# Loads of a fused RWKV and SoLU kernel moved from one DMA queue to three

## The chip, the cores and the metric

The kernel runs on one core of a Trainium2 chip. The metric is the time of one launch on the device in microseconds. Over the two runs of the kernel before, it is 154.34 us (median; 154.29 and 154.40).

Five engines work side by side, each through its own list of instructions, in order: PE (TensorE, matrix products), DVE (VectorE), ACT (ScalarE), POOL (GpSimd) and SP (SyncE). SP computes nothing here; it issues DMA transfers between the device memory and the on-chip memory. An engine waits at an instruction until the semaphores that it names have been reached, and everything behind it on that engine waits too.

## The reference

Two stages, in float32. First a recurrence over 768 positions for 4 batches and 8 heads of width 48:

```python
for t in range(S):
    cur = np.einsum('bhd,bhe->bhde', u[None] * kt, vt)
    y[:, :, t] = np.einsum('bhd,bhde->bhe', rt, state + cur)
    state = wt[:, :, :, None] * state + np.einsum('bhd,bhe->bhde', kt, vt)
```

Then, with `x` the 3072 x 384 rows of `y`, a hidden layer of 1024 with SoLU, a norm over its columns, and the way back to 384:

```python
h = x @ w_in
sm = softmax(h)             # over the 1024 columns
solu = h * sm
ln = (solu - mean(solu)) / np.sqrt(var(solu) + 1e-06) * g_ln
out = ln @ w_out
```

## The kernel before

The 768 positions are cut into 6 chunks of 128, so with 4 batches there are 24 units of work, numbered 0 to 23 (`units`, chunk by chunk). For a unit the four inputs w, k, r and v are each loaded as a tile of 128 positions by 8 heads by 48 numbers in float32: 192 KB, in rows of 192 bytes, 1024 rows to a tile.

All work is written out by hand in the string `ORDER` (lines 21 to 67). A word is a stage, a unit and sometimes a letter or digit that says which engine or PSUM bank: `vb3.p` is the stage `vb` of unit 3 on POOL. Each word calls a function, and the wrapper `InOrder` (lines 72 to 90) makes the instructions of each engine follow one another in just the order in which the words stand. Line 86 in that wrapper is where nearly every instruction is recorded, so the profile gives L86 for nearly all; a group is told by its tiles.

The words that matter here:

- `LW`, `LK`, `LR`, `LV` (lines 246 to 256) load w, k, r, v of a unit, all on SP. `LU`, `LG`, `LI`, `LO` load u, g and the two weight matrices; `out` (line 536) stores a finished unit. v has 7 buffers (`NIO`), unit i taking buffer i modulo 7.
- `lw` (ACT) takes the logarithm of w; `cum` (PE) sums it along the chunk; `ex` (ACT) takes exponents; `kp` (DVE, `scaled` at line 333) multiplies k and r with them.
- `p` and `q` (POOL) multiply k with r and with u; `qh` (POOL) halves q by an addition for some units; `dg` (DVE) sums q per head; `dv` (POOL) multiplies that sum with v.
- `vb` (POOL, ACT or DVE by its letter) casts v to bfloat16. It is the only reader of a loaded v tile.
- `M`, `m`, `sel`: scores on PE, their copy on ACT or DVE, the mask of some units on POOL. `Y` (PE) and `y` (ACT or DVE) make the output of the recurrence out of m, vb, dv and the state; `S`, `et`, `st` carry the state on.
- `X`, `xT`, `H`, `e`, `he`, `hq`, `ea`, `Oa`, `Ob`, `sq`, `qm`, `lv`, `o`: the second stage; `ea` (POOL) adds the two halves of e.
- `gw`, `ce`, `mn`, `mc`, `wi`: the weights, once.

How the readers of v stand: for units 3, 4, 6, 7, 10, 12 and 14 `vb` is on POOL; for 5, 8, 11 and 13 on DVE; for 9 on ACT. In `ORDER` the word `LV` of a unit stands ahead of its `vb`, often directly ahead: `LV3 vb3.p dv3 sel4`, `LV4 vb4.p`, `LV14 vb14.p`. Where `LV` is on SP that closeness means little, since SP goes through its own words ahead of the others.

Of the kernel before, what the change touches and what calls it, by code (L numbers as in the profile page):

```python
# [8 lines left out]
F32 = mybir.dt.float32  # L9
BF16 = mybir.dt.bfloat16  # L10
# [11 lines left out]
LW2 LU0 ik0 lw2 hot5.4 cum2.0 LW1 lw1 us0.7 ih0 LW3 lw3 cum3.2 LR2 uc0 ex2 LK2 p2 LV2 vb2.p kp2 hot4.4 krk2.6 krr2  # L22
LR1 LK1 cum1.4 LW0 ex1 kp1 kr2.d hot1.0 S2.7 lw0 et2 LV1 vb1.d LW4 st2 p1 q1 hot2.0 krk1.1 krr1 q2 qh2 dg2 LG0
kr1.a M2.4 ex3 hot1.0 M1.6 m1.d dv2 LR0 LK0 p0 q0 cum0.0 ex0 lw4 cum4.6 ex4 kp0 krk0.1 krr0 LR3 gs0.0 gc0 dg1
m2.d Y2.i0 kr0.d LK3 p3 LR4 LV0 vb0.a dg0 dv1 kp3 Y1.i5 hot3.1 krk3.4 krr3 LK4 kp4 M0.2 m0.d krk4.1 y1.a X1.5
krr4 y2.a X2.0 dv0 xT2.d hot1.6 Y0.n7 y0.d kr3.a M3.2 hot1.0 X0.6 S1.4 p4 q3 kr4.a xT1.a xT0.a LI2 LI1 wi1.a
M4.0 m4.a et1 LI0 S0.5 et0 wi0.d m3.d LO1 wi2.p H1.6 e1 gw5.a H2.0 e2 H0.2 LO0 gw2.a q4 qh4 dg4 qh3 dg3 gw4.p
gw7.p LV3 vb3.p dv3 sel4 LW6 e0 gw6.d st1 LV4 vb4.p he1 lw6 dv4 gw1.d LW5 gw0.d gw3.d mn0.4 mc0 ce5.p ce6.p
Y3.i7 ce4.p he2 st0 he0 cum6.0 y3.a ce7.p hot1.5 X3.6 lw5 xT3.a ce3.d LK6 LR6 p6 Y4.n5 LR5 LK5 ce2.d hq0.a ex6
LW7 cum5.2 H3.6 p5 y4.d ex5 ce1.d ce0.d Oa0.5 kp6 krk6.1 krr6 S4.0 hq1.d Oa1.4 kp5 krk5.3 krr5 X4.2 Ob1 e3 he3  # L30
LV5 q6 q5 kr5.d hq2.a et4 st4 M5.6 kr6.a M6.0 xT4.d lw7 cum7.2 hq3.a sq1 m6.a m5.d dg5 vb5.d qm1 dv5 Ob0 ex7 sq0
qm0 S3.7 qh6 LR7 LK7 p7 kp7 et3 lv1 st3 lv0 H4.0 Y5.n6 y5.d LR9 LK8 o1.d e4 krk7.3 krr7 Oa2.2 he4 X5.7 q7 kr7.d
LW9 lw9 o0.a LK9 p9 LW8 lw8 S5.6 et5 cum9.4 ex9 Ob2 sq2 LR8 p8 st5 dg6 kp9 qm2 LV6 xT5.a LV9 vb6.p dv6 sel6
cum8.0 ex8 kp8 hq4.a LV7 LV11 out1 LW10 dg7 vb7.p dv7 Oa3.3 vb9.a lv2 H5.6 e5 M7.4 m7.d he5 q8 krk9.1 LK10 krr9
kr9.a S9.0 et9 Ob3 sq3 st9 q9 qm3 o2.a out0 ea5.p Y6.i5 y6.a LV8 LR10 Y7.n4 y7.d LW11 LW12 krk8.1 M9.6 lw10 lv3
X6.2 xT6.a m9.d o3.a krr8 LV10 out3 out2 kr8.d qh9 dg9 dg8 hq5.d cum10.4 ex10 kp10 S6.0 vb11.d et6 X7.2 xT7.a
st6 p10 vb8.d dv8 dv9 H6.6 e6 he6 H7.2 lw11 e7 he7 M8.4 m8.a Oa5.1 Y9.n0 Ob5 sq5 y9.d cum11.6 ex11 krk10.5 krr10
qm5 kr10.d S7.4 et7 st7 Oa4.3 hq6.d lv5 lw12 o5.a X9.2 sel8 Y8.i0 vb10.p y8.a LK11 LR11 kp11 xT9.d q10 dg10 p11
M10.4 m10.a sel10 S10.1 et10 st10 dv10 S8.0 et8 S11.7 et11 X8.6 xT8.a LK12 LW13 cum12.4 q11 ex12 lw13 st11 st8
Ob4 sq4 qm4 LW14 LR12 kp12 p12 lw14 lv4 o4.a out5 LK13 LV12 LR13 Y10.n2 dg11 y10.d H8.6 e8 krk12.1 krk11.0 krr11  # L40
krr12 kr12.d he8 kr11.a q12 qh12 cum13.4 H9.2 vb12.p S12.1 ex13 p13 q13 ea7.p dg12 kp13 dv11 LW16 LR14 LK14 e9
he9 et12 st12 M12.6 m12.a Oa6.0 X10.5 xT10.a krk13.4 krr13 kr13.a M11.6 m11.d ea8.p dv12 sel12 p14 cum14.2 ex14
q14 out4 Ob6 sq6 hq8.d M13.4 m13.d LV13 hq7.a LW15 lw15 lw16 kp14 vb13.d H10.6 dg13 qm6 LW18 lw18 Y11.n1 y11.d
Oa8.5 LK16 LR15 LR16 LK15 e10 he10 hq9.a krk14.4 Y12.i3 krr14 lv6 qh14 kr14.d p15 ea10.p dv13 LR18 LV14 vb14.p
q15 qh15 LK18 p18 Ob8 sq8 qm8 y12.a S13.2 et13 st13 o6.a lv8 X11.1 xT11.d cum16.6 ex16 X12.3 hq10.d LW19 kp16
Oa9.4 cum15.0 xT12.a Ob9 ex15 kp15 sq9 o8.a dg14 dv14 qm9 M14.2 m14.a sel14 krk16.7 Oa7.6 krr16 kr16.d lv9 o9.d
cum18.0 ex18 kp18 Ob7 LV15 S14.5 et14 st14 krk15.3 krr15 kr15.d LK19 Y13.i2 lw19 cum19.0 krk18.7 p16 q16 vb15.a
S15.4 y13.a sq7 qm7 dg15 X13.5 xT13.d ex19 LR19 kp19 lv7 o7.a q18 krr18 kr18.d H11.2 et15 st15 krk19.5 krr19
kr19.d LW17 lw17 cum17.0 e11 he11 ex17 ea11.p out8 LK17 LR17 p17 kp17 H12.6 e12 he12 hq11.a p19 H13.4 e13 Oa10.3
Y14.n2 M16.0 m16.a dg16 q19 dv15 y14.d ea12.p ea13.p M15.6 m15.d he13 Ob10 sq10 X14.2 out9 Oa11.1 LW20 qm10 lw20  # L50
cum20.6 hq12.d krk17.0 krr17 out6 out7 LV16 vb16.a dv16 xT14.a S16.2 LR20 ex20 LK20 dg18 et16 st16 lv10 o10.a
H14.4 e14 kp20 Ob11 sq11 kr17.d LK23 qm11 lv11 o11.a Oa12.2 krk20.3 krr20 kr20.a he14 sel16 Y16.n7 y16.d Y15.n6
y15.d M19.4 m19.a M18.0 m18.d Ob12 X15.7 xT15.a q17 hq13.d LV19 LW21 LV17 X16.3 xT16.a ea14.p vb19.a M17.4 m17.d
sq12 LK22 out10 qm12 dg17 qh19 vb17.p sel19 p20 hq14.a LW22 LV20 q20 qh20 dv17 M20.0 LV21 m20.d out11 LK21 H15.6
e15 he15 lw22 ea15.p H16.4 LV18 vb18.p dv18 LR21 p21 lw21 Oa14.3 Y17.n1 LR22 LV23 q21 dg19 dv19 Ob14 LR23 p23
p22 e16 he16 lv12 Oa13.0 LW23 o12.a out12 sq14 qm14 hq15.d vb20.a lv14 dg20 dv20 y17.d cum21.6 ex21 Ob13 cum22.4
sq13 ex22 LV22 vb22.p ea16.p o14.d out14 Y18.n2 y18.d Oa15.1 X18.3 qm13 kp22 lv13 xT18.d X17.2 xT17.a kp21 Ob15
sq15 qm15 S18.5 et18 st18 Y19.n4 y19.d lv15 o15.a out15 o13.a krk22.2 S17.3 et17 lw23 H18.6 e18 ea18.p hq16.d
vb21.d st17 Y20.n5 y20.d X19.4 xT19.d krr22 kr22.a H17.0 he18 hq18.d cum23.4 ex23 kp23 Oa16.3 e17 ea17.p he17
krk21.2 krr21 kr21.a H19.6 e19 krk23.5 X20.4 krr23 q22 qh21 vb23.p out13 xT20.a kr23.a he19 Oa18.2 Ob16 sq16  # L60
M21.0 q23 ea19.p qh23 dg22 dv22 m21.a sel21 qm16 lv16 M22.6 hq19.a M23.4 Ob18 sq18 dg21 H20.0 o16.a out16 m22.d
m23.d Oa19.7 Y22.n6 qm18 lv18 hq17.d Ob19 S19.5 dg23 dv23 e20 Oa17.4 y22.d X22.3 he20 et19 st19 xT22.d dv21
Y21.n6 Ob17 y21.d sq19 o18.a sq17 qm17 lv17 Y23.n1 out18 qm19 lv19 X21.0 xT21.d H22.2 o17.a e22 out17 ea20.p
y23.d H21.0 X23.5 xT23.a e21 hq20.d o19.d out19 Oa20.6 he22 hq22.d H23.4 e23 he21 hq21.d Ob20 sq20 qm20 lv20
o20.a out20 ea22.p Oa22.7 ea21.p Oa21.3 he23 hq23.d Ob22 sq22 qm22 lv22 Ob21 sq21 qm21 lv21 o21.d o22.a out22
out21 ea23.p Oa23.2 Ob23 sq23 qm23 lv23 o23.a out23
"""

NIO, NLW, NKP, NWK = 7, 10, 6, 4
# [24 lines left out]
def kernel(  # L94
# [26 lines left out]

    nc.scalar.preload_act_table_set("natural_log_exp_and_others")
# [32 lines left out]
    g_rows = consts.tile([KF, 128], F32)  # L155

# [57 lines left out]
    qm_t = ring("qm", NWK, [C, 1], F32)  # L214
    lv_t = ring("lv", NWK, [C, 1], F32)
# [30 lines left out]
    def load_w(i, x):  # L246
        sp.dma_start(out=w_t[i % NIO][:, :, :D], in_=rows_of(w, i))

    def load_k(i, x):
        sp.dma_start(out=kr_t[i % NIO][:, 0, :, :D], in_=rows_of(k, i))  # L250

    def load_r(i, x):
        sp.dma_start(out=kr_t[i % NIO][:, 1, :, :D], in_=rows_of(r, i))

    def load_v(i, x):
        sp.dma_start(out=v_t[i % NIO][:, :, :D], in_=rows_of(v, i))

    def load_u(i, x):
        sp.dma_start(out=u_row, in_=u.rearrange("(o h) d -> o (h d)", o=1))

    def load_g(i, x):
        sp.dma_start(out=g_rows, in_=moe_g_ln.rearrange("(ko ki) -> ko ki", ki=128))

    def load_w_in(j, x):
        sp.dma_start(out=win_f[:, j, :], in_=moe_w_in[j * 128:(j + 1) * 128, :])

    def load_w_out(j, x):
        part = slice(j * KF // 2, (j + 1) * KF // 2)
        sp.dma_start(out=wout_f[:, part, :],
                     in_=moe_w_out.rearrange("(ko ki) d -> ki ko d", ki=128)[:, part, :])  # L270
# [109 lines left out]

    def scores(i, x):
        kr = kr_s[i % NKP]
        m_ps = live[i]["m_ps"] = bank([C, 2, HP, C], F32, x, "m_ps")
        for hp in range(HP):
            for a in range(2):
                rows = slice(64 * a, 64 * a + 64)
                pe.matmul(m_ps[:, a, hp, :], lhsT=kr[rows, hp, :], rhs=kr[rows, HP + hp, :], start=True, stop=True)
# [80 lines left out]

    def hidden(i, x):
        xT = xT_t[i % NWK]  # L470
        h_ps = live[i]["h_ps"] = bank([128, KF, C], F32, x, "h_ps")
# [4 lines left out]

    def hidden_exp(i, x):
        act.activation(out=e_t[i % NWK], in_=live[i]["h_ps"], func=EXP)
# [7 lines left out]
    def hidden_mul(i, x):  # L486
        dve.tensor_mul(out=he_t[i % NWK], in0=live[i]["h_ps"], in1=e_t[i % NWK])

    def hidden_square(i, x):
        he, hq = he_t[i % NWK], hq_t[i % NWK]  # L490
        if x == "a":
            act.activation(out=hq, in_=he, func=SQUARE)
        else:
            (dve if x == "d" else pool).tensor_mul(out=hq, in0=he, in1=he)

    def output(i, part):
        L = live[i]
        e, he, hq, o_ps = e_t[i % NWK], he_t[i % NWK], hq_t[i % NWK], L["o_ps"]
        for f in range(part * KF // 2, (part + 1) * KF // 2):
            pe.matmul(o_ps[:, :DM + 1], lhsT=he[:, f, :], rhs=w2[:, f, :], start=(f == 0), stop=False,  # L500
# [16 lines left out]

    def sums(i, x):
        act.activation(out=sq_t[i % NWK], in_=live[i]["o_ps"][:, DM:DM + 2], func=SQUARE)

    def variance(i, x):
        dve.tensor_sub(out=qm_t[i % NWK], in0=live[i]["o_ps"][:, DM + 2:], in1=sq_t[i % NWK][:, 0:1])
# [61 lines left out]
```

## Time and profile before

| | |
|---|---|
| time, median of two runs | 154.34 us |
| span of the profiled execution, first to last instruction | 152.4 us |
| time less span | 1.9 us |
| PE busy | 136.4 us (90%) |
| DVE busy | 131.8 us (87%) |
| ACT busy | 120.0 us (79%) |
| POOL busy | 119.0 us (78%) |
| DMA queue of SP, share of the 16 DMA engines' span | 77.4% |
| bytes moved | 27.06 MB, of 104,825 packets 100,314 under 512 B |

The page gives each engine's busy time over one profiled execution. Matrix products are pipelined, so a busy PE is not a PE at its peak. The DMA share counts the time that the packets took on the 16 DMA engines. A unit of a row like `x24` is the number of such instructions; the numbers behind the bar are total busy time and the mean of one; what follows in brackets is how long the engine stood idle ahead of it and whom it waited for.

| stretch, us | PE | DVE | ACT | POOL | DMA share |
|---|---|---|---|---|---|
| 25 to 43 (18.0 long) | 15.27 | 17.04 | 15.08 | 14.28 | 1.03 |
| 43 to 60 (17.0 long) | 16.94 | 16.73 | 15.73 | 13.05 | 0.94 |
| 60 to 75 (15.0 long) | 15.00 | 14.29 | 13.77 | 13.04 | 0.97 |
| 75 to 90 (15.0 long) | 14.22 | 14.65 | 13.35 | 14.74 | 0.96 |
| 90 to 110 (20.0 long) | 19.54 | 19.78 | 18.73 | 18.34 | 0.94 |
| 110 to 130 (20.0 long) | 19.68 | 19.61 | 17.28 | 17.82 | 0.44 |

### The profile page before, as it was taken

How to read it: one execution, taken by the hardware profiler on the slowest of the kernel's cores; microseconds unless marked ns; L12 is line 12 of the kernel's file. 1: busy time of each engine (PE TensorE's matmuls, PEld its weight loads, DVE VectorE, ACT ScalarE, POOL GpSimd, SP SyncE). 2: the span in 40 equal slices, each digit the busy share in tenths (PEclk: the TensorE clock that was granted, in tenths of full speed). 3: DMA queues.
4: the chain of work that ended last, by engine and by line, in shares of the span. 5: the costliest groups of instructions: out<-in, count | busy, mean ns of one | idle time of the engine just before them, and what ended most of it. 6: DMA issues, size and time to landing. Idle time of an engine off the chain costs nothing.

```text
span 152.4 us, 5172 instructions
## 1 busy us (share of the span) xinstructions
PE 136.4 (90%) x2093; PEld 105.5 (69%) x2093; DVE 131.8 (87%) x227; ACT 120.0 (79%) x247; POOL 119.0 (78%) x149
## 2 busy tenths in 40 slices
PE   6777598968999999999998999999799999999970
PEld 1242365936778889779776689887686988889740
DVE  5029968899999999998999999999999999988940
ACT  4526648869888999799998889998988789938661
POOL 7268986799909994899999997799889979973600
PEclk9959969999999999999999999999999999999998
DMA  3999999989979999989897989995998110112023
GB/s 76 218 216 211 217 334 377 254 175 223 216 151 216 220 204 229 206 177 224 194 203 144 228 195 275 199 199 136 241 205 210 63 45 4 44 63 103 4 79 127
DMA packets 104825, 27.06 MB, mean 178 GB/s; under 512 B 100314, under 2 KB 104419, under 8 KB 104803
## 3 DMA queue, kind: packets, MB, share of 16 engines
q1 hardware_dynamic: 104802, 26.75, 77.4%
q8 instruction: 16, 0.26, 0.7%
q14 instruction: 7, 0.05, 0.1%
HBM read 22.03 MB, written 4.72 MB: 176 GB/s over the span
## 4 chain that ended last, share of the span: by engine, by line
PE 53%; DVE 23%; SPq 8%; ACT 6%; issue 3%; DMA 2%; POOL 1%; DVEq 0%; POOLq 0%
PE ps L86 53%; SPq L86 7%; DVE he L86 6%; DVE m L86 4%; DVE kp L86 4%; DVE w L86 3%; DMA kr_in<-in_k_dram 2%; DVE kr L86 1%; DVE hq L86 1%; DVE y L86 1%; DVE st L86 1%; ACT ps L86 1%; ACT o L86 1%; DVE dg L86 1%; ACT win_sb L86 1%
## 5 line engine op out<-in xcount | busy, mean ns | idle before, releaser
L86 PE MATMUL ps<-w,he 128*128 128x385 bf16 x192 | 44.5, 325 | 1.0 <-DVE w L86 0.7
L86 PE MATMUL ps<-xT,win_sb 128*128 128x128 bf16 x576 | 35.5, 219 | 1.1 <-DVE qm L86 0.8
L86 PEld LDWEIGHTS <-win_sb 128*128 128x128 bf16 x576 | 32.8, 98 | 2.2 <-DVE m L86 0.9
L86 PE MATMUL ps<-one_col,hq 128*128 128x1 bf16 x192 | 31.5, 164 | 0.0
L86 DVE TENSOR_TENSOR he<-ps,e 128x1024 bf16<-128x1024 f32 x24 | 29.1, 1214 | 1.6 <-ACT e L86 1.6
L86 DVE TENSOR_TENSOR kp<-ps,kr_in 128x768 bf16<-128x768 f32 x24 | 22.8, 951 | 7.7 <-DMA kr_in<-in_k_dram 4.9
L86 POOL TENSOR_TENSOR p<-kr_in 128x384 bf16<-128x384 f32 x24 | 24.7, 1038 | 4.5 <-DMA kr_in<-in_k_dram 4.2
L86 POOL TENSOR_TENSOR dv<-vb,dg 128x384 bf16<-128x384 bf16 x24 | 21.7, 907 | 7.5 <-DVE qm L86 3.6
L86 ACT ACTIVATE e<-ps 128x1024 bf16<-128x1024 f32 x24 | 24.5, 1021 | 3.1 <-PE ps L86 2.0
L86 POOL TENSOR_TENSOR ea<-e 128x512 bf16<-128x512 bf16 x17 | 20.0, 1181 | 6.4 <-ACT e L86 5.7
L86 POOL TENSOR_TENSOR q<-p,u_bc 128x384 bf16<-128x384 bf16 x24 | 22.2, 931 | 2.4 <-DVE dg L86 1.7
L86 ACT ACTIVATE ps<-ps 128x768 f32<-128x768 f32 x24 | 19.1, 799 | 5.1 <-PE ps L86 4.3
L86 PEld LDWEIGHTS <-kp 128*128 128x128 bf16 x272 | 17.5, 100 | 6.0 <-DVE kp L86 3.2
L86 PEld LDWEIGHTS <-he 128*128 128x128 bf16 x192 | 18.4, 96 | 4.0
L86 PEld LDWEIGHTS <-hq 128*128 128x128 bf16 x192 | 15.4, 96 | 8.3
L86 DVE TENSOR_TENSOR m<-ps,keep 128x1024 bf16<-128x1024 f32 x15 | 18.2, 1216 | 1.2 <-PE ps L86 1.0
L86 PE MATMUL ps<-ident,kp 128*128 128x128 bf16 x192 | 16.5, 227 | 1.6 <-POOL p L86 1.1
L86 DVE TENSOR_TENSOR hq<-he 128x1024 bf16<-128x1024 bf16 x15 | 13.4, 890 | 0.1
L86 ACT COPY kr<-ps 128x1024 bf16<-128x1024 bf16 x11 | 11.1, 1012 | 2.4 <-PE ps L86 2.4
L86 ACT ACTIVATE lw<-w_in 128x384 bf16<-128x384 f32 x23 | 11.7, 523 | 1.3 <-DMA w_in<-in_w_dram 1.3
L86 PEld LDWEIGHTS <-kr 64*128 64x128 bf16 (+1 forms) x272 | 10.2, 95 | 3.1 <-ACT kr L86 0.7
L86 PE MATMUL ps<-inv_col,ea 128*128 128x1 bf16 x68 | 11.2, 165 | 0.0
(90 smaller groups left out, 293.7 us busy)
## 6 DMA issues: line engine op xcount, KB each, us to landing
w_in<-in_w_dram SPq DMA_DIRECT2D x24, 192.0 KB, 3.7
kr_in<-in_r_dram SPq DMA_DIRECT2D x24, 192.0 KB, 3.7
kr_in<-in_k_dram SPq DMA_DIRECT2D x24, 192.0 KB, 3.7
v_in<-in_v_dram SPq DMA_DIRECT2D x24, 192.0 KB, 3.6
out_dram<-o SPq DMA_DIRECT2D x24, 192.0 KB, 2.6
win_f<-in_moe_w_in_dram SPq DMA_DIRECT2D x3, 512.0 KB, 6.4
wout_f<-in_moe_w_out_dram SPq DMA_DIRECT2D x2, 768.0 KB, 9.0
u_row<-in_u_dram SPq DMA_DIRECT2D x1, 1.5 KB
```

The source lines that it names most:

```text
L86: made = make(*args, **kwargs)
```

## The change

A load word may now carry a letter that picks the queue that issues it: none for SP, `a` for ACT, `g` for POOL.

```diff
+    queue = {"": sp, "a": act, "g": pool}
...
     def load_k(i, x):
-        sp.dma_start(out=kr_t[i % NIO][:, 0, :, :D], in_=rows_of(k, i))
+        queue[x].dma_start(out=kr_t[i % NIO][:, 0, :, :D], in_=rows_of(k, i))
...
     def load_v(i, x):
-        sp.dma_start(out=v_t[i % NIO][:, :, :D], in_=rows_of(v, i))
+        queue[x].dma_start(out=v_t[i % NIO][:, :, :D], in_=rows_of(v, i))
```

In `ORDER` four loads move to the head and to ACT, ahead of `lw2`, the first work of ACT:

```diff
-LW2 LU0 ik0 lw2 hot5.4 cum2.0 LW1 lw1 us0.7 ih0 LW3 lw3 cum3.2 LR2 uc0 ex2 LK2 p2 LV2 vb2.p kp2 ...
-LR1 LK1 cum1.4 LW0 ... dv2 LR0 LK0 p0
+LW2 LU0 ik0 LK2.a LK1.a LV2.a LR0.a lw2 hot5.4 cum2.0 LW1 lw1 us0.7 ih0 LW3 lw3 cum3.2 LR2 uc0 ex2 p2 vb2.p kp2 ...
+LR1 cum1.4 LW0 ... dv2 LK0 p0
```

The loads of v of units 3 to 14 keep their places in the string and go to POOL:

```diff
-gw7.p LV3 vb3.p dv3 sel4 LW6 e0 gw6.d st1 LV4 vb4.p he1
+gw7.p LV3.g vb3.p dv3 sel4 LW6 e0 gw6.d st1 LV4.g vb4.p he1
...
-Ob2 sq2 LR8 p8 st5 dg6 kp9 qm2 LV6 xT5.a LV9 vb6.p dv6 sel6
+Ob2 sq2 LR8 p8 st5 dg6 kp9 qm2 LV6.g xT5.a LV9.g vb6.p dv6 sel6
```

and in the same way `LV5.g`, `LV7.g`, `LV11.g`, `LV8.g`, `LV10.g`, `LV12.g`, `LV13.g`, `LV14.g`. In the built program the list of POOL around the twelve loads is, in its order: `gw7`, **LV3**, `vb3`, `dv3`, `sel4`, **LV4**, `vb4`, `dv4`, four `ce`, `p6`, `p5`, **LV5**, `q6`, `q5`, `dv5`, `qh6`, `p7`, `q7`, `p9`, `p8`, **LV6**, **LV9**, `vb6`, `dv6`, `sel6`, **LV7**, **LV11**, `vb7`, `dv7`, `q8`, `q9`, `ea5`, **LV8**, **LV10**, `qh9`, `p10`, and further on `p12`, **LV12**, `q12`, `qh12`, `vb12`; `q14`, **LV13**, `qh14`; `dv13`, **LV14**, `vb14`, `q15`. SP has 16 instructions fewer, ACT four more and POOL twelve more. The load of r of unit 0 on ACT carries a wait for the load of w of unit 2 (the two share a completion semaphore), and stands ahead of `lw2`.

The rest of the diff changes no instruction: the last step of `lv` gets a word of its own (`rs`), which stands directly behind it, so ACT's order is the same; two small rings of tiles are added; and functions for other ways to turn tiles are added that no word calls.

## The prediction

> **What bounds the kernel now.** I read the page first: busy times and the chain of waits.
>
> ```profile
> PE 136.4 (90%) x2093; PEld 105.5 (69%) x2093; DVE 131.8 (87%) x227; ACT 120.0 (79%) x247; POOL 119.0 (78%) x149
> ...
> PE 53%; DVE 23%; SPq 8%; ACT 6%; issue 3%; DMA 2%; POOL 1%; DVEq 0%; POOLq 0%
> ```
>
> PE and DVE carry 76% of the chain, SP's queue 8%, POOL 1%. The 8% of SP is the start: the chain in order of time runs through SP's issues from 0.79 to 13.31 us, then through the landing of k of unit 3 to 17.14. From 43 us on it is PE and DVE, and the stretches leave DVE 0.27 us idle of 17, 0.71 of 15, 0.35 of 15, 0.22 of 20. Whatever makes DVE late after 43 us stays late to the end.
>
> The start in SP's own timeline (start, length, queue, what), and the stretch it lies in (length, then busy time of PE, weight loads, DVE, ACT, POOL, clock, DMA share, GB/s):
>
> ```profile
> 4.09 0.85 SPq L86 DMA_DIRECT2D kr_in<-in_k_dram  x1
> 4.98 0.99 SPq L86 DMA_DIRECT2D v_in<-in_v_dram  x1
> 6.01 0.76 SPq L86 DMA_DIRECT2D kr_in<-in_r_dram  x1
> 6.81 0.85 SPq L86 DMA_DIRECT2D kr_in<-in_k_dram  x1
> ```
>
> ```profile
> 3.80:15.00 11.20, 8.35 (x59) 4.00 (x58) 4.50 (x7) 5.29 (x10) 6.13 (x12) 0.85 1.08 215
> ```
>
> A load holds SP for about 0.85 us, but the first one of all, with no traffic ahead, for 0.43. Meanwhile the DMA engines are full (share 1.08) at 215 GB/s, which is 0.91 us per load of 192 KB. So SP issues at the rate at which the DMA engines drain, and is not itself the limit.
>
> Then POOL's timeline where the first moved load will stand:
>
> ```profile
> 29.96 0.50 POOL L86 CAST vb<-v_in 128x384 bf16<-128x384 f32 x1 [0.25 <-DMA v_in<-in_v_dram]
> 30.55 0.94 POOL L86 TENSOR_TENSOR dv<-vb,dg 128x384 bf16<-128x384 bf16 x1
> 31.45 1.21 POOL L86 TENSOR_SCALAR_AFFINE_SELECT m<-m 128x1024 bf16<-128x1024 bf16 x1
> 32.61 0.62 POOL L86 CAST vb<-v_in 128x384 bf16<-128x384 f32 x1
> 33.31 0.83 POOL L86 TENSOR_TENSOR dv<-vb,dg 128x384 bf16<-128x384 bf16 x1
> ```
>
> These are `vb3 dv3 sel4 vb4 dv4`, without a gap. SP had issued v3 at 20.97 and v4 at 24.99, long before. In the changed list POOL issues v3 only when it has come to 29.7 and reads it in its next instruction. What a landing takes is in the view of the tile v_in:
>
> ```profile
> L86 SPq DMA_DIRECT2D v_in<-in_v_dram x24: 378/760/4108, 5.0 to 114.8; - x24
> ...
> DMA to landing us min/median/max: 3.1/3.6/6.7
> ```
>
> **Part 1, four loads on ACT.** Removed from SP's chain: 0.85 + 0.99 + 0.85 + 0.37 us, with gaps 3.2 us. If issuing were the limit, that would be the gain. By the full DMA engines it is not: up to k of unit 3 the same 16 loads must pass at 0.91 us each, so it lands at 17.1 as before, and the gain is 0. The Trainium skill (DMA: Bandwidth & Descriptors, "Issuing engines are not separate DMA queues") says so too: several issuing engines save only the sequencer's issue time. Against it the skill (Perfetto Trace Analysis, "DMA Optimizations") would balance the issuers where descriptor generation is the bottleneck; by that one the sum falls by these 3.2 us.
>
> What part 1 costs: ACT, free at 2.07 after its table load, issues three loads (0.43 to 0.99 each), waits for w of unit 2 (landed 3.43), issues the fourth, and only then starts `lw2`, at 3.9 to 6.0 instead of 3.43. Behind it stand `lw1`, `lw3`, `uc0`, `ex2`. Loads of two queues would share the DMA engines, so w3, in at 5.79, could come 1.7 later (two loads of ACT served in between) and r2, which `kp2` needs, about 1.5 later. That is a loss of up to 2 us for unit 2. `p3` at 17.41 is what the chain goes through, with POOL idle 0.07 us ahead of it, so POOL's two units of work before it could carry such a loss on. I take 0, between a gain of 3.2 and a loss of 2.
>
> **Part 2, twelve loads on POOL.** The trace has no DMA issued by POOL. Call i the time that one holds POOL, L the time from its start until the tile is there. Bounds of i: 0.4 us (SP's free issue, 0.43) and 3.6 (SP's slow end, 4.11, short of one). I take 1.0, nearest to what POOL's other instructions last (0.50 to 1.21). L: at least 3.1 (shortest landing), at most 6.7 (longest); I take i + 3.1 = 4.1. Nothing hides this on POOL: `vb` stands next, and behind it `dv`, `sel`, `p`, `q` of the following units, for which PE and DVE wait. POOL's own lag D grows; the lag of DVE and PE is D less the slack at each hand-over, read from the starts and ends of before.
>
> - v3, v4: 2 L, less 0.25 that `vb3` waited already and 0.36 idle at the first `ce`. D = 7.6. Then v5 ahead of `q6 q5`: + i, D = 8.6. `q5` ended at 41.80, `dg5` on DVE began at 44.54: slack 2.74. DVE lags 5.9, and since `dv5` waits for that DVE work, so does POOL.
> - v6, v9, then `vb6`: + L (v9 is issued while v6 flies): 10.0. v7, v11, then `vb7`: + L: 14.1.
> - v8, v10 stand ahead of `qh9`: + 2 i = 16.1. The next rows (timeline of all engines) show a hand-over without slack, and the last one of the sum:
>
> ```profile
> 57.21 0.55 POOL L86 TENSOR_TENSOR q<-q 128x192 bf16<-128x192 bf16 x1
> ...
> 58.03 0.80 DVE L86 TENSOR_REDUCE dg<-q 128x8 f32<-128x192 bf16 x2
> ...
> 80.36 1.00 DVE L86 CAST vb<-v_in 128x384 bf16<-128x384 f32 x1
> ...
> 81.22 0.91 POOL L86 TENSOR_TENSOR q<-p,u_bc 128x384 bf16<-128x384 bf16 x1
> ```
>
>   `qh9` ended 57.76, `dg9` began 58.03: slack 0.27. DVE lags 15.8. POOL's 2.66 us of idleness at 58.7 is used up by this.
> - v12 has `q12 qh12` (1.6 us) between itself and `vb12`: + max(i, L - 1.6) = 2.5. D = 18.3.
> - v13 is issued behind `q14`, which ended at 82.13; but DVE read it (`vb13`) at 80.36. So DVE lags D + L + 1.8 = 24.2, with `dg13`, `y11`, `he` queued behind.
> - v14 costs POOL L, but the hand-overs after it (`q15` 88.11 to `dg15` 91.26, `dv14` 89.85 to `y14` 98.16) have 3 to 8 us, and POOL itself waits for `dg13`: 0.
>
> Sum 24.2, kept to the end because DVE has no idle time to give. SP's list loses work and its loads run further ahead: no gain, since nobody waits for them after the start. The execution of 152.4 becomes 176.6; the median lies 1.9 above its span, so 178.5, told as 178.
>
> With the lower bounds (0.4, 3.1) the same steps give 3.5, + 3.1, + 3.9 less 0.3, + 1.5, + 4.9 = 16.6: 171. With the upper ones (3.6, 6.7): 13.7, 20.9, 35.0, 40.1, 48.6: 203.
>
> **Rivals.**
>
> *The lag dies on slack.* If buffers ahead of DVE and PE take up all but the first two stalls and v13 is not late, 5.9 is left: 160. For it: hand-overs of units 13 to 18 have 3 to 8 us. Against it: those of units 5 to 12 have 0.3 to 2.7. Chance 0.08.
>
> *One issue holds POOL for long.* One load is 1024 rows of 192 bytes; if POOL needs 3.6 us for each, 203. For it: POOL takes 0.5 us even for the cast of one such tile, and SP has been held 4.11 us by one load of v. Against it, SP manages in 0.4 when nothing is ahead. The Trainium skill (SBUF — State Buffer, "SBUF: two separate sides") has a rule for it: a DMA from GpSimd starves while DVE holds the shared port, in its example about 620 ns becoming 3100. Here DVE is busy 98% of 43 to 60 us; no run so far shows a DMA of POOL beside it. Chance 0.17.
>
> *Faster.* POOL's sequencer runs ahead of its arithmetic and issues the loads as early as SP did, with v3 landed before 29.96; then part 2 is free, and if the start was bound by issuing, 3.2 comes off: 151.1. The point from which it decides: DVE stays on time as long as POOL is late by less than 2.74 us at `q5` and 0.27 at `qh9`. Against it: nothing in the trace shows POOL starting a row before the one ahead has ended, and 3.1 is the shortest landing. Chance 0.04.
>
> *No difference.* Early issue on POOL as above and nothing gained at the start: 154. Chance 0.03.
>
> **How the numbers follow.** The forecast, 178, has 0.68; its own spread is 168 (lower bounds and 3.2 gained at the start) to 190. The slack case (160) and the two early-issue cases lie on the low side with 0.15 together, the long hold on the high side with 0.17, most of it below 200. A range from 164 to 200 leaves out about 0.2. About 2% (3 us) is what a measurement tells from no change. Slower by over 2%: 0.68 + 0.17 + 0.08 = 0.93; within 0.03; faster 0.04, though that one sits near its edge.
>
> **What would show it.** In the profile after: POOL rows `vb<-v_in` waiting for the DMA v_in, about 3 us each for units 3, 4, 6, 7, and DVE's cast for unit 13 with a wait of several us; POOL in the chain of waits instead of SP, or DMA v_in as a link there; DVE's idle time up by some 20 us, in 30 to 110. At the start: k of unit 3 read by POOL at about 17.4, `lw2` later than 3.43. Wrong would be: `vb3` without a wait, an unstretched stretch of 43 to 75, or twelve DMA rows on POOL that last far under 0.4 or over 3.6 us each.

## The result, and the profile after

| | before | after |
|---|---|---|
| time, median | 154.34 us | 179.72 us (178.71 to 180.72) |
| ratio, 95% interval | | 1.1664 [1.1574, 1.1754] |
| span of the profiled execution | 152.4 us | 177.0 us |
| mean granted clock of PE | 0.975 | 0.907 |

A time here is the median over all launches of a kernel; a ratio leaves out those more than 1.5% above the kernel's fastest, so it can differ a little from the quotient of two times.

The kernel is 16.6% slower: 24.6 us of span. The page of the changed kernel: busy times, the queues of POOL (q0) and ACT (q10) with packets, MB and share of the 16 DMA engines' span, and the shares of the chain of waits:

```profile
PE 145.9 (82%) x2091; PEld 111.8 (63%) x2093; DVE 129.9 (73%) x227; ACT 121.4 (69%) x247; POOL 129.7 (73%) x161
...
q0 software_dynamic: 768, 2.36, 4.3%
q10 hardware_dynamic: 4160, 0.79, 2.2%
...
PE 32%; POOL 24%; DVE 13%; issue 10%; SPq 7%; DMA 7%; ACT 4%; POOLq 0%; DVEq 0%
```

DVE has no more work than before (129.9 us after 131.8), but 73% of the span instead of 87%: it now waits. POOL has 24% of the chain, where it had 1%, DMA 7% instead of 2%; POOL's own work grew by 10.7 us, near the twelve issues of 0.93 us (11.2).

The view of the tile v_in gives the new instructions, who is idle for them, and the time from issue to landing over all loads of v:

```profile
L86 POOL DMA_DIRECT2D v_in<-in_v_dram x12: 884/930/1119, 29.1 to 106.1; - x12
...
  POOL vb L86: 15.8, 6
...
  DVE vb L86: 4.4, 1
  ACT vb L86: 4.2, 1
...
DMA to landing us min/median/max: 2.8/3.6/5.3
```

An issue holds POOL for 0.93 us, and six casts of POOL wait 15.8 us together for the data. POOL's timeline at the place of `vb3 dv3 sel4 vb4`, which ran without a gap before:

```profile
29.11 1.12 POOL L86 DMA_DIRECT2D v_in<-in_v_dram  x1
33.99 0.50 POOL L86 CAST vb<-v_in 128x384 bf16<-128x384 f32 x1 [3.76 <-DMA v_in<-in_v_dram]
34.57 0.83 POOL L86 TENSOR_TENSOR dv<-vb,dg 128x384 bf16<-128x384 bf16 x1
35.35 1.09 POOL L86 TENSOR_SCALAR_AFFINE_SELECT m<-m 128x1024 bf16<-128x1024 bf16 x1
36.40 0.93 POOL L86 DMA_DIRECT2D v_in<-in_v_dram  x1
40.44 0.50 POOL L86 CAST vb<-v_in 128x384 bf16<-128x384 f32 x1 [3.12 <-DMA v_in<-in_v_dram]
```

POOL issues the load, then stands idle until it has landed: 4.88 us from the start of the issue to the cast for v3, 4.04 for v4. DVE's timeline shows the same lateness handed on (the bracket is the idle time ahead and its releaser): first for `y4`, which needs `dv4`, later for `dg9`, which needs `qh9`, and at the cast of unit 13, whose load POOL had issued at 100.98:

```profile
41.89 0.56 DVE L86 TENSOR_TENSOR y<-ps,dv 128x384 bf16<-128x384 f32 x1 [6.58 <-POOL dv L86]
...
73.16 0.81 DVE L86 TENSOR_REDUCE dg<-q 128x8 f32<-128x192 bf16 x2 [2.77 <-POOL q L86]
...
104.10 0.66 DVE L86 CAST vb<-v_in 128x384 bf16<-128x384 f32 x1 [4.40 <-DMA v_in<-in_v_dram]
```

From 30 to 105 us DVE is idle for 25.6 of 75 us; the same work before, from 30 to 81, left it 1.0 idle of 51. So the whole loss lies in these stretches: the last long stretch of PE in the chain, 601 products, starts at 135.10 instead of 110.34 and takes the same 37.24 us (37.23).

### The profile page after: what moved, and what is told of

Its sections match the earlier page's. It is cut to its first block, busy times and chain, and to the rows that moved or that the text cites. A ratio compares the mean times of both kernels' runs of the same rounds, so it can differ in the third digit from the quotient of the medians.

```text
span 177.0 us, 5181 instructions
## 1 busy us (share of the span) xinstructions
PE 145.9 (82%) x2091; PEld 111.8 (63%) x2093; DVE 129.9 (73%) x227; ACT 121.4 (69%) x247; POOL 129.7 (73%) x161
## 3 DMA queue, kind: packets, MB, share of 16 engines
q10 hardware_dynamic: 4160, 0.79, 2.2%
## 4 chain that ended last, share of the span: by engine, by line
PE 32%; POOL 24%; DVE 13%; issue 10%; SPq 7%; DMA 7%; ACT 4%; POOLq 0%; DVEq 0%
PE ps L86 32%; SPq L86 7%; POOL q L86 6%; POOL v_in L86 4%; DMA v_in<-in_v_dram 4%; POOL dv L86 4%; POOL p L86 4%; DMA kr_in<-in_k_dram 3%; DVE m L86 3%; DVE he L86 3%; DVE kp L86 2%; POOL m L86 2%; DVE kr L86 2%; DVE dg L86 2%; POOL w L86 1%
## 5 line engine op out<-in xcount | busy, mean ns | idle before, releaser
L86 PE MATMUL ps<-w,he 128*128 128x385 bf16 x192 | 46.7, 336 | 0.0
L86 PE MATMUL ps<-xT,win_sb 128*128 128x128 bf16 x576 | 37.5, 225 | 1.2 <-DVE qm L86 0.8
L86 PEld LDWEIGHTS <-win_sb 128*128 128x128 bf16 x576 | 34.9, 102 | 2.5 <-DVE m L86 1.0
L86 PEld LDWEIGHTS <-kp 128*128 128x128 bf16 x272 | 18.3, 103 | 14.9 <-issue 10.0
L86 PEld LDWEIGHTS <-hq 128*128 128x128 bf16 x192 | 16.1, 99 | 9.6 <-issue 2.1
L86 PE MATMUL ps<-ident,kp 128*128 128x128 bf16 x192 | 17.3, 233 | 1.0 <-DVE kp L86 0.9
L86 POOL CAST vb<-v_in 128x384 bf16<-128x384 f32 x12 | 6.1, 511 | 15.8 <-DMA v_in<-in_v_dram 15.8
L86 DVE TENSOR_TENSOR y<-ps,dv 128x384 bf16<-128x384 f32 x17 | 9.3, 551 | 9.0 <-POOL dv L86 8.4
L86 PE MATMUL ps<-vb,kp 128*128 128x96 bf16 x80 | 7.0, 212 | 9.1 <-ACT vb L86 3.3
L86 PEld LDWEIGHTS <-kr 64*128 64x128 bf16 (+1 forms) x272 | 10.9, 99 | 4.1 <-issue 1.7
```

The costliest lines, as they stand in the source:

```text
L86: made = make(*args, **kwargs)
```

## The experiments

Line 86 of the two kernels stands at line 85 in these, since `ORDER` has one line fewer. "Changed kernel" is the one after. Ratios are against the kernel before on the same chip (154.95 us beside the first four, 155.38 beside the next four, 154.29 beside the last two), with their 95% interval.

**Each part alone.** First the four loads on ACT, all of v on SP as before; then the twelve on POOL, the first four on SP:

```diff
-LW2 LU0 ik0 lw2 hot5.4 ... LR2 uc0 ex2 LK2 p2 LV2 vb2.p ... LR1 LK1 cum1.4 ... dv2 LR0 LK0 p0
+LW2 LU0 ik0 LK2.a LK1.a LV2.a LR0.a lw2 hot5.4 ... LR2 uc0 ex2 p2 vb2.p ... LR1 cum1.4 ... dv2 LK0 p0
```

> Part 1 alone: four first loads on ACT, all loads of v on SP as before. Theory (the loss is made by POOL waiting for v, the start is bound by the DMA engines): no difference, 152.5 to 156 us. Rival 'SP's issuing was the limit at the start': 151 us or less. Rival 'the start pays for the loads on ACT': 156 us or more.

Measured 154.96 us, ratio 1.0022 [0.9997, 1.0047], span 153.2. The time stays, but not because the loads pass as before. The DMA engines moved 234 GB/s in 3.8 to 15.0 instead of 215 (share 1.17 after 1.08), and k of unit 3 was issued at 11.60 instead of 13.35. The view of its tile, for that one issue:

```profile
L85 SPq DMA_DIRECT2D kr_in<-in_k_dram x1: 973/973/973, 11.6 to 11.6; - x1
...
DMA to landing us min/median/max: 3.6/3.6/3.6
```

So it landed at 15.2, about 1.9 us earlier than 17.14. Against that stands the first unit: `kp2` began at 8.94 instead of 7.77, since r of unit 2 took 6.0 us to land, and the logarithm of w of unit 3 at 7.17 instead of 5.79. The chain of waits now goes through that landing, `p3` starts at 18.09 instead of 17.41 without waiting for a load, and the gain on k of unit 3 does not reach the end.

```diff
-gw7.p LV3 vb3.p dv3 sel4 ... LV4 vb4.p
+gw7.p LV3.g vb3.p dv3 sel4 ... LV4.g vb4.p
...
```

> Part 2 alone: loads of v of units 3 to 14 on POOL at their old places, the first loads on SP as before. Theory: all of the loss, 177 to 182 us. Rival 'both parts share it': 174 us or less.

Measured 180.47 us, 1.1644 [1.1588, 1.17], span 177.3. Part 2 alone makes the whole loss, and part 1 adds nothing to it.

**The same twelve issues on POOL, but earlier.** The changed kernel with its load words moved ahead in `ORDER`, `LV5.g` staying (each line: the words around the new place):

```diff
-q4 qh4 dg4
+LV3.g LV4.g q4 qh4 dg4
...
-LV5.g q6 q5 kr5.d
+LV5.g q6 q5 LV6.g LV9.g LV7.g LV8.g kr5.d
...
-LK7 p7 kp7
+LK7 LV11.g p7 kp7
...
-st6 p10 vb8.d
+st6 p10 LV10.g LV12.g LV13.g vb8.d
...
-vb12.p S12.1
+vb12.p LV14.g S12.1
```

> Both parts, but the loads of v on POOL stand several words earlier in its list, in gaps where it was idle, so that each tile has landed when its reader comes; the same twelve issues, by the same queue. Theory (the waits for landing make the loss, the issues themselves cost little): 153 to 158 us, no wait of the casts of v for DMA. Rival 'holding POOL makes the loss' (12 x 0.93 us): about 165 us. Rival 'the transfers of this queue are slow or slow the others': 170 us or more.

Measured 157.26 us, 1.0172 [1.0131, 1.0213], span 155.5: 21.5 of the 24.6 us are gone with the queue, the engine and the number of issues unchanged. The view of the tile v_in, and one place of POOL's timeline where four issues stand back to back:

```profile
L85 POOL DMA_DIRECT2D v_in<-in_v_dram x12: 884/928/1088, 24.3 to 75.4; - x12
...
  DMA v_in<-in_v_dram: 0.6, 1
```

```profile
43.20 3.70 POOL L85 DMA_DIRECT2D v_in<-in_v_dram  x4
```

An issue takes what it took, 0.93 us, and one wait of 0.6 us for v is left, for unit 5, whose load stayed at its place. So the loss comes with the place of the issue, directly ahead of its reader, and not with POOL's queue or the number of issues. The rest, 1.7%, is under the 2% that the prediction takes as the least that can be told from no change, and was not taken apart; POOL is busy 17.70 of 18 us from 25 to 43 there, and 16.72 of 17 from 43 to 60.

**The holding alone.** v on SP as before, part 1 kept, and at each of the twelve places POOL does a cast of 128x900 that nobody reads, sized to last as long as an issue:

```diff
-LV3.g vb3.p
+LV3 hold3 vb3.p
...
+    def hold(i, x):
+        pool.tensor_copy(out=idle_o, in_=wout_f.rearrange("p a n -> p (a n)")[:, 1536:2436])
```

> Part 1, the loads of v on SP as before, and at each of the twelve places POOL does instead a cast of 128 x 900 numbers into a tile that nobody reads, about 0.93 us, as long as an issue holds it. Measures the holding alone. Theory: the same sum with L = i = 0.93, that is 5 to 6 us: 158 to 162 us. Rival 'holding makes the loss': 175 us or more. Rival 'holding is free': 153 to 156 us.

Measured 161.85 us, 1.048 [1.0424, 1.0536], 6.9 us more than before; the twelve casts took 0.94 us each at the median. That is somewhat above the 5 to 6 us expected, and 28% of the 24.6 us: holding POOL at these places costs something, waiting for the landing the greater part. POOL's lateness reaches DVE here too, at the hand-overs without slack, in the waits of DVE:

```profile
DVE dg L85 <- POOL q L85: 3.0, 1, 3.0
...
DVE y L85 <- POOL dv L85: 2.4, 1, 2.4
```

**One term at a time.** The last term: the changed kernel with only the load of v13 moved, from behind `q14` to directly behind `vb12`:

```diff
-vb12.p S12.1 ... M13.4 m13.d LV13.g hq7.a
+vb12.p LV13.g S12.1 ... M13.4 m13.d hq7.a
```

> The changed kernel with one word moved: the load of v of unit 13 stands directly behind the cast of v of unit 12 on POOL instead of behind q of unit 14. Tests the last term of the sum (DVE's cast of unit 13 waits for it). Theory: the wait of 4.4 us on DVE goes, POOL's lag of about 18.9 us stays and decides: 4 to 6 us less than the changed kernel, 173.5 to 176.5 us. Rival 'POOL would have made DVE just as late anyway': 178 to 181 us.

Measured 175.52 us, 1.1231 [1.116, 1.1302], span 172.3: 4.7 us of span come back with one word. DVE's cast of unit 13 no longer waits:

```profile
99.92 1.01 DVE L85 CAST vb<-v_in 128x384 bf16<-128x384 f32 x1
```

It stands at 99.92 instead of 104.10. The first term: the kernel before with only v3 and v4 on POOL.

```diff
-gw7.p LV3 vb3.p dv3 sel4 ... LV4 vb4.p
+gw7.p LV3.g vb3.p dv3 sel4 ... LV4.g vb4.p
```

> The kernel before with only the loads of v of units 3 and 4 on POOL at their old places. Tests the first term. Theory: two landings of about 4.1 us, less 0.25 that the cast waited already and 2.4 of slack up to the addition of y of unit 4 on DVE: 5.5 us, kept to the end: 159 to 161.5 us. Rival 'a lag this early dies on slack later': 154 to 157 us.

Measured 161.64 us, 1.0418 [1.0359, 1.0477], 6.3 us more, 0.1 above the range expected. The waits of POOL and DVE (us in total, times, longest):

```profile
DVE y L85 <- POOL dv L85: 7.2, 1, 7.2
...
POOL vb L85 <- DMA v_in<-in_v_dram: 6.7, 2, 3.4
```

Two waits of 3.4 and 3.3 us on POOL, from 32 and 38 us on, become 6.3 us at the end, more than 100 us later: nothing downstream gives it back.

**Is it POOL?** The kernel before with the same twelve words on ACT instead, at the same places:

```diff
-gw7.p LV3 vb3.p dv3 sel4 ... LV4 vb4.p
+gw7.p LV3.a vb3.p dv3 sel4 ... LV4.a vb4.p
...
```

> The kernel before with the twelve loads of v at their old places but on ACT's queue, whose issues are made as SP's are. Theory (late issue by an engine that goes through its own work in order, with the reader close behind, is the loss, whatever the queue): clearly slower, 158 to 172 us, with waits of the casts of v for DMA. Rival 'it is POOL's kind of transfer': 153.5 to 156 us.

Measured 168.0 us, 1.0735 [1.0645, 1.0825], span 166.0. ACT's issue of v3, and the cast on POOL that reads it:

```profile
30.60 0.42 ACTq L85 DMA_DIRECT2D v_in<-in_v_dram  x1
...
34.86 0.50 POOL L85 CAST vb<-v_in 128x384 bf16<-128x384 f32 x1 [4.49 <-DMA v_in<-in_v_dram]
```

An issue is 0.37 us at the median and stands in ACT's queue, not in POOL's, and POOL still waits 4.49 us for v3, 11.0 us for v in all. An engine that works through its words in order, POOL or ACT, issues a load only when it comes to the word; what made the old places harmless was that SP has no other work. The loss is 7.4% here and 16.4% from POOL. One reason is in the trace: ACT casts neither v3 nor v4, so it issued v4 at 31.94, 1.3 us after v3, and `vb4` did not wait, while on POOL the issue of v4 stands behind `vb3`. The rest of that difference was not taken apart.

**The start on POOL.** Three variants of the kernel before that change only the first loads. Two loads of k behind `LU0` and one of r behind `ih0`:

```diff
-LW2 LU0 ik0 lw2 ... ih0 LW3 ... ex2 LK2 p2 ... LR1 LK1 cum1.4 ... LR0 LK0 p0
+LW2 LU0 LK2.g LK1.g ik0 lw2 ... ih0 LR0.g LW3 ... ex2 p2 ... LR1 cum1.4 ... LK0 p0
```

> The kernel before, with k of units 2 and 1 and r of unit 0 issued by POOL at the start, when it has only constants to make; all v on SP. POOL's transfers took 768 packets for 12 loads where SP's took 1024 packets for one, and about two thirds of the time on the DMA engines. Theory (start bound by the DMA engines, cheaper transfers relieve it): units 1 and 2 begin 0.5 to 1.5 us earlier; the total 152.5 to 154.5 us. Rival 'the start is hidden behind DVE's work on the weights': 154 to 155.5 us. Rival 'POOL's constants come too late': 155.5 us or more.

Measured 154.34 us beside 155.38, 0.9933 [0.9897, 0.9968], span 152.3. Unit 1 came earlier (`p1` at 9.89 instead of 10.51), unit 2 later (8.48 instead of 7.79), unit 3 at the same time (17.43). Half of the expectation fell; the interval leaves out 1, but 0.7% is under the 2% that a measurement can tell from no change, and its cause is open. So unit 2 was tried by itself, and then with unit 0:

```diff
-LW2 LU0 ik0 lw2 ... cum3.2 LR2 uc0 ex2 LK2 p2
+LW2 LU0 LK2.g LR2.g ik0 lw2 ... cum3.2 uc0 ex2 p2
```

> The kernel before, with k and r of unit 2 issued by POOL at 2.7 us, ahead of the rest of its constants; everything else on SP. With k of units 2 and 1 and r of unit 0 on POOL, r of unit 2 (still on SP) landed at 8.3 us, 5.5 after its issue, and held the first product of unit 2. Theory (that landing was late because the transfers of POOL's queue went through in turn with SP's, so both tiles of the first unit belong on the same queue): first product of k and r of unit 2 at 6.5 to 7.5 us instead of 7.8; total 152.5 to 154.5 us. Rival 'the start before 17 us does not reach the end': 154 to 155.5 us.

Measured 154.53 us, 1.0027 [0.9988, 1.0065]: `p2` at 8.40, where 6.5 to 7.5 was expected. The load of r that POOL had issued at 3.81 took 4.4 us to land, and `p2` waited for it. So the expected reason, that both tiles belong on one queue, is not borne out.

```diff
-ih0 LW3 ... vb2.p kp2 ... LR0 LK0 p0
+ih0 LR0.g LW3 ... vb2.p LK0.g kp2 ... p0
```

> As the last, and r and k of unit 0 on POOL too, in its idle time after its constants and after the cast of v of unit 2. Four loads less in SP's chain and on the costlier kind of packets. Theory: k of unit 3 lands 1 to 2 us earlier than 17.1, total 152 to 154 us. Rival 'the start before 17 us does not reach the end': 154 to 155.5 us. Rival 'two issues hold POOL ahead of its products of units 1 and 2': 155.5 us or more.

Measured 154.52 us, 1.0069 [1.0028, 1.0111]. k of unit 3, issued at 11.44, landed 3.6 us later, at 15.0, 2.1 us earlier than before, as expected. `gw4` and `gw7` began at 26.14 instead of 27.25, and the end did not move with it: at the start, who issues a load changes places among units, not the time. No run gave a version that is clearly faster than the kernel before.

## Why the prediction was right

It said 178 us, 164 to 200, slower with 0.93; 179.72 was measured. The mechanism of part 2 stands by the runs: earlier issues take away 21.5 of 24.6 us, and part 2 alone makes the loss. For part 1 only the number was right, and in part 2 some steps met their number by luck. The steps against the two traces, each lag the start of the same instruction after less before:

| hand-over | before, us | after, us | lag, us | predicted, us |
|---|---|---|---|---|
| `dg5` on DVE | 44.54 | 50.57 | 6.0 | 5.9 |
| `vb6` on POOL | 50.57 | 60.86 | 10.3 | 10.0 |
| `vb7` on POOL | 52.98 | 66.53 | 13.6 | 14.1 |
| `dg9` on DVE | 58.03 | 73.16 | 15.1 | 15.8 |
| `vb12` on POOL | 72.42 | 91.31 | 18.9 | 18.3 |
| `vb13` on DVE | 80.36 | 104.10 | 23.7 | 24.2 |
| last stretch of 601 products on PE | 110.34 | 135.10 | 24.8 | 24.2 |

- **The first row is met by another path.** The step had `q5` make DVE late by POOL's lag less a slack of 2.74. In the trace `q5` ended at 50.07, half a microsecond before `dg5` began, and `dg5` did not wait for it. DVE was late by then, 5.3 us through `dv4`, for which `y4` waited, and 6.0 through the products of PE behind `vb4` (which ended at 40.95), for which `kr5` waited. The chain of waits, start and length:

```profile
40.99 7.08 PE ps L86 x84
...
48.09 0.69 DVE kr L86
```

  So the issue of v5, priced at 1.0, made DVE no later there. The granted clock was 0.70 in 40.9 to 48.1 us, which no step had. That 6.0 came out beside 5.9 is luck.
- **The two prices.** One issue was taken at 1.0 us and took 0.93; issue to cast was taken at 4.1 and took 4.88, 4.04, 4.27, 3.26, 5.31 and 3.12 for v3, v4, v6, v7, v12 and v13, mean 4.15. Neither had a row in the trace of before; the nearest rows were enough. At the first load two errors nearly cancel: POOL came to it at 29.11 instead of 29.7, and it took 4.88 instead of 4.1, so `vb3` was late by 4.0 where the sum has 3.9.
- **Two terms are off, and cancel by luck.** v12 was given 2.5 us and cost 3.8, since its load took 5.31 us to land; v13 was given 5.9 and cost 4.8, since its landing took 3.12. The 4.2 us that ACT's cast of unit 9 waits is in no step. It held `e5` behind it, and with that `he5` on DVE, whose lag went from 6.0 to 10.3 us; the later hand-overs from POOL took DVE further (12.2 at `y7`, 15.1 at `dg9`), so it does not show at the end.
- **The sum of the lower bounds** begins with 3.5, which leaves out the 0.25 that `vb3` had waited already; with it the sum is 16.4, still 171 us.
- **Part 1** was put at 0 between a gain of 3.2 and a loss of 2, and the time agrees (1.0022), but the step behind the 0 failed. By full DMA engines k of unit 3 was to land at 17.1 as before, since the loads up to it (counted as sixteen; they are fifteen of 192 KB and two small ones) must pass at 0.91 us each. In the changed kernel it was issued at 11.41 and landed 3.4 us later, at 14.8, and the DMA engines moved 240 GB/s in 3.8 to 15.0: 215 was not the most that they could do. The loss came as the step had it: `lw2` at 4.26, in the 3.9 to 6.0 given, `lw3` at 7.02, 1.2 us late where 1.7 was the most, and `kp2` 1.1 us late (8.89 instead of 7.77), near the 1.5. No step worked out that this gain and this loss come out even at the end; that is luck. Nor was it so that nobody waits for SP's loads after the start: `gw4` on POOL had waited 1.74 us for the second weight matrix, began at 26.49 instead of 27.25 now that SP came to it earlier, and that is why POOL was early at v3. And the step had ACT issue only from 2.07, after its table load. ACT in the changed kernel:

```profile
0.79 1.28 ACT L124 ACT_TABLE_LOAD   x1 [0.79 <-PEq L613]
0.82 0.48 ACTq L83 DMA_DIRECT2D kr_in<-in_k_dram  x1
1.33 0.70 ACTq L86 DMA_DIRECT2D kr_in<-in_k_dram  x1
2.06 1.03 ACTq L86 DMA_DIRECT2D v_in<-in_v_dram  x1
3.84 0.37 ACTq L86 DMA_DIRECT2D kr_in<-in_r_dram  x1
4.26 0.52 ACT L86 ACTIVATE lw<-w_in 128x384 bf16<-128x384 f32 x1 [2.19 <-DMA w_in<-in_w_dram]
```

  The issues began at 0.82, beside the table load. `lw2` was 0.8 us late: its own input, w of unit 2, was there only by 3.84 instead of 3.43, and the fourth issue, which waits for it too and stands ahead, took the rest. The rule of the Trainium skill that the step was weighed with (DMA: Bandwidth & Descriptors, "Issuing engines are not separate DMA queues"), by which only issue time is saved, agrees with SP's list, where k of unit 3 was issued 1.9 us earlier. Its rule for balancing the issuers (Perfetto Trace Analysis, "DMA Optimizations") was to take 3.2 us off, and the time stayed; whether SP's long rows were descriptor generation, no run here shows.
- **The rival "dies on slack" fell**: two stalls alone keep 6.3 us to the end, and the later ones add to them.
- **The rival "one issue holds POOL for long" fell**: 0.88 to 1.12 us, and the same twelve holds without a late load cost 6.9 us. The Trainium skill (SBUF — State Buffer, "SBUF: two separate sides") has a DMA of GpSimd starve while VectorE holds the port that the two share. The trace of the early issues does not show it: with DVE busy 3.11 of the 3.70 us, the four issues back to back took 0.925 us each. Whether VectorE held that port then, no run shows.
- **The rivals "faster" and "no difference"** needed POOL to issue ahead of its arithmetic. It did not: each issue stands in the timeline between the instructions that the list has around it.
- **What no step had: the clock.** In the changed kernel the granted clock is lower around PE's long waits: 0.50 in 35 to 41 us, where PE is busy 2.51 of 6, and 0.66 in 60 to 75, where it is busy 10.73 of 15, beside 1.00 in 75 to 90, where it is busy 13.13 of 15. What PE does there takes longer: a product `ps<-w,he` takes 0.48 us at 44.88 and 0.32 at 45.26. The same 79 products of the chain, first in the kernel before, then in the one after:

```profile
83.53 6.06 PE ps L86 x79
```

```profile
106.94 7.40 PE ps L86 x79
```

  The stretch rows around them (length, busy time of PE, weight loads, DVE, ACT, POOL, clock, DMA share, GB/s) give 1.00 and 0.79 for the clock:

```profile
83.50:89.60 6.10, 6.07 (x83) 4.35 (x83) 5.75 (x12) 5.00 (x12) 6.02 (x8) 1.00 1.14 237
```

```profile
106.90:114.40 7.50, 7.46 (x84) 4.97 (x84) 5.82 (x12) 5.19 (x12) 5.03 (x8) 0.79 0.31 79
```

  That is 1.3 us, about what the lag grows from `vb13` (23.7) to the last stretch of PE (24.8). It offset the sum's 0.5 too many at `vb13`. It was not tried by itself. The Trainium skill (TensorE: Matmul & The Clock Gate, Part 1) has the clock go to half after an idle window of about 3.4 us; the trace agrees with the half in 35 to 41 us (0.50), though the two waits of PE there, 2.70 and 3.03 us, are each shorter than that window.

What stays open: how part 1's earlier k and later first unit come to cancel, how the 1.7% of the early-issue kernel divides between POOL's holding and anything else, and the 0.7% of the first variant of the start.

## What to carry to other kernels

A load's place in a hand-written order means something only on an engine that has other work: on an idle issuing engine it runs ahead by itself, on a working one the issue is part of the sequence, and it has to stand a landing time (here 4 us) ahead of its reader. Before moving an issue, find who reads the tile next and what that engine is doing in between; and price each stall at the next hand-over by the slack there, since on a kernel whose engines are full it stays to the end. A step that meets its number can still have the wrong path: look in the trace for what each hand-over waited for. And before spreading the first loads over queues, find the unit that the chain goes through: here one tile landed about 2 us earlier, the first unit came 1 us later, and the time stayed.

## What the runs showed of the hardware that was not expected

- POOL's queue carried the twelve loads in 768 packets, 64 to a load, 3072 bytes or 16 rows of 192 bytes each; ACT's four loads took 4160 packets, some 1024 to a load, one per row. By the shares of the page, one load occupied the 16 DMA engines for 0.63 us from POOL (4.3% of 177.0 over 12) and for 0.97 from ACT (2.2% over 4). The early-issue kernel did not turn that into time.
- An issue occupies POOL's arithmetic for 0.93 us, but ACT issues beside its own work: in the changed kernel at 0.82 us, while its table load ran from 0.79 to 2.07.
- With k and r of unit 2 issued by POOL at 2.69 and 3.81 us (before, SP issued them the other way round at 2.86 and 4.09), r landed only 4.4 us after its issue began, and `p2`, which waited for it, started at 8.40, 0.6 us later than before. A queue of its own gave that load no precedence; why was not settled.
